# Clustered attention followed by an MLP on one core: a mask product and three ScalarE operations placed in other periods

## The chip, the cores and the metric

The kernel runs on one core of a Trainium2 chip. Its time is the device time of that core in microseconds, from launch to the last write. Before the change three runs were measured: 1022.56, 1022.64 and 1022.86 us. A further execution was recorded by the hardware profiler.

The core's engines each work through their own instructions in order and meet only through semaphores: TensorE (PE in the profile; its loading of weights is listed apart as PEld), VectorE (DVE), ScalarE (ACT), GpSimd (POOL), and SyncE (SP), which here only starts transfers.

## The reference

For 4 batches and 8 heads, 768 tokens with 64 values each, every query and every key is assigned to the nearest of 16 centroids of its head. A query may look only at keys with the same assignment. Then the result goes through an MLP with 2048 hidden values and the gate h * erf(softplus(h)).

```python
q_assign = np.argmax(np.einsum('bhsd,hcd->bhsc', q_n, c_n), axis=-1)
k_assign = np.argmax(np.einsum('bhsd,hcd->bhsc', k_n, c_n), axis=-1)
mask = q_assign[:, :, :, None] == k_assign[:, :, None, :]
scores = scale * np.matmul(q, k.transpose(0, 1, 3, 2))
scores = np.where(mask, scores, -1000000000.0)
scores = scores - np.max(scores, axis=-1, keepdims=True)
attn = np.exp(scores)
attn = attn / (np.sum(attn, axis=-1, keepdims=True) + 1e-09)
return np.matmul(attn, v).astype(np.float32)
...
h = x @ w_in
sp = np.maximum(h, 0.0) + np.log1p(np.exp(-np.abs(h)))
g = h * erf(sp)
return (g @ w_out).astype(np.float32)
```

## The kernel before

**Two parts.** The first part, up to about 430 us of the span, is the attention. The second is the MLP, made of products of 128x128 blocks into PSUM banks called `bank`. The change touches the first part only.

**Pairs and periods.** The attention runs over 16 pairs of heads (`p`, 0 to 15). The two heads of a pair lie on partitions 0 to 63 and 64 to 127, so most TensorE products come in twos: one contracts over rows 0 to 63 (`e` = 0), the next over rows 64 to 127 (`e` = 1). A pair has six periods (`i`, 0 to 5), and a period treats two units; a unit is 128 keys against half of the queries (384 of 768). `period(p, i)` (line 720) writes out the order by hand, and a wrapper class (`InOrder`, line 55) keeps every engine's instructions in the order in which the code calls them. All of them therefore carry line 63 in the profile, and the groups are told apart by their tiles.

**One period on TensorE**, in this order:

- in periods 0 and 3 `turn` (line 390): six small products that turn the row minima (`lowest`) into the bank `turned[h]`. Two ScalarE copies then write them as one row for each head into `qm`, the masks of the queries. `scores` read that row.
- `step_ahead` (line 711): a step of the row maxima for the pair ahead, four short bf16 products into `wide` (from `kv`, `qv`, then `km`, `qm`). VectorE reduces `wide` to `nmx`, and the next step writes the same `wide` again. From period 3 on these steps belong to the next pair.
- place 0 of a mask product (`mask(0)`).
- `products` (line 410) of the two units: `qT` times `kT` in f32 into a bank `sc`.
- place 1 of a mask product, and a second `step_ahead`.
- `scores` (line 423) of the two units: four short bf16 products of `km` and `qm` onto the same `sc`.
- place 2 of a mask product. Its copy by ScalarE stands between the `curve` of the first unit and that of the second.
- in period 3, `similarities` for the pair after the next, into `turned[1]`.
- `attend` (line 453) of the two units of the period before: `pr` times `in_v` into `turned[half]`. In the profile these are the `turned<-pr,in_v` products over all 128 rows.
- in periods 0 and 3 the beginning of `divide` (line 465): the sums of the weights (`minus` times the accumulated `pr`) into the other bank `turned[1 - half]`.

**Mask products.** `masks` (line 350) multiplies the one-hot assignments `hotT` with `pick`, over rows 0 to 63 for the queries and 64 to 127 for the keys, into a bank `turned`. ScalarE copies the result to `qm` (queries) or `km` (keys, with a bias). There are four per pair: two halves for each of queries and keys. The table `MASKS` (line 51) says in which period and place each stands, and for the pair after the current one; `FIRST_MASKS` is the same for pair 0. The bank is `turned[0]` in periods 0 and 5, `turned[1]` otherwise. Before, both key products stand in period 0, at places 1 and 2. The row maxima of the next pair read the second half of its `km` for the first time at the second `step_ahead` of period 3.

**ScalarE in a period** does the copies of the turn, the copy of a mask if there is one, two `curve` operations (the exponential from `sc` to `pr`), and then, in periods 0 and 3, the two operations of `divide`, Ln and Exp, which make `inv`. In the period that follows VectorE makes from them `den` (reading the bank of the sums), then the scaled accumulator, then, after a row maximum, the result `x`. The next `attend` writes the bank that `den` reads.

**The conversion.** The MLP's weights arrive as 64-bit numbers and are turned into f32 by integer and f32 operations, one piece of 512 columns at a time, 22 of 32 pieces during the attention: pieces 2p-1 and 2p in pair p (`n1`, `n2`; with none for -1). A piece takes `size_and_rest` (line 236, two ScalarE operations: Abs into `w_in`, and a scaled copy of the low word), `bounded` (VectorE), `sign` (line 245, ScalarE, written as int16 into the upper half of the low words), `shifted` (VectorE) and `summed` (line 253, POOL, which adds the parts and then fetches a later piece into the place that came free). `sign` follows the `size_and_rest` of its piece, and `summed` follows all.

**POOL** adds up the `pr` of each unit (`accumulate`) and runs `summed` in periods 1 and 4.

Of the kernel before, what the change touches and what calls it, by code (L numbers as in the profile page):

```python
# [47 lines left out]
NPT = NJ + 2  # L48
N_LATE = 10
LAST_X = 11  # L50
MASKS = {(0, 1): ("k", 0), (0, 2): ("k", 1), (2, 0): ("q", 0), (5, 0): ("q", 1)}
FIRST_MASKS = {(2, 0): ("k", 0), (2, 1): ("q", 0), (2, 2): ("k", 1), (5, 0): ("q", 1)}


# [17 lines left out]
def kernel(  # L72
# [163 lines left out]
    def size_and_rest(n):  # L236
        w, (hi, lo, _) = w_steps[n][0], steps[n]
        ae.activation(out=w, in_=hi, func=ACT.Abs, scale=UP)
        ae.activation(out=lo.bitcast(I32), in_=lo.bitcast(U32), func=ACT.Copy, scale=2.0**-29)

    def bounded(n):
        w = w_steps[n][0]
        ve.tensor_scalar(out=w, in0=w, scalar1=2.0, scalar2=None, op0=ALU.max)

    def sign(n):
        hi, _, upper = steps[n]
        ae.activation(out=upper, in_=hi, func=ACT.Prelu, scale=2.0**-25, alpha=2.0**90)

    def shifted(n):
        w = w_steps[n][0].bitcast(U32)  # L250
        ve.tensor_scalar(out=w, in0=w, scalar1=3, scalar2=None, op0=ALU.logical_shift_left)
# [59 lines left out]
    def similarities(p):  # L311

        if p >= NPAIR:
            return
        st = pairs[p]
        st["psim"] = turned[1][:, 0:HW]
        for g in range(4):
            te.matmul(
                st["psim"][2 * C * g : 2 * C * (g + 1)], lhsT=ccT[:, p % HP],
                rhs=st["qk"[g // 2] + "T"][:, (g % 2) * HW : (g % 2 + 1) * HW],  # L320
                start=True, stop=True,
            )

    def choose(p, spare=None):

        if p >= NPAIR:
            return
        st = pairs[p]
        n = HW // C
        sims = routep.tile([P, HW], F32, name="sims")  # L330
        ve.transpose(out=sims, in_=st.pop("psim"))
        yield
        sim = sims.rearrange("p (g c) -> p g c", c=C)
        mx = (wide[:, 0] if spare is None else spare)[:, 512 - n :]
        ve.reduce_max(out=mx, in_=sim, axis=AX.X)
        yield
        hot = routep.tile([P, HW], BF16, name="hot")
        ve.tensor_tensor(
            out=hot.rearrange("p (g c) -> p g c", c=C), in0=sim,
            in1=mx.unsqueeze(2).to_broadcast([P, n, C]), op=ALU.is_equal,  # L340
        )
        yield
        st["hotT"] = routep.tile([P, HW], BF16, name="hotT")
        ve.transpose(out=st["hotT"], in_=hot)
# [5 lines left out]
    def masks(p, nm, half, bank):  # L350

        if p >= NPAIR:
            return lambda: None
        st = pairs[p]
        cols = slice(half * HW, (half + 1) * HW)
        r = slice(0, D) if nm == "q" else slice(D, P)
        won = bank[:, 0:HW]
        te.matmul(won, lhsT=pick[r, half], rhs=st["hotT"][r], start=True, stop=True)
        if nm == "q":
            return lambda: ae.activation(out=st["qm"][:, cols], in_=won, func=ACT.Relu)  # L360
        return lambda: ae.activation(
            out=st["km"][:, cols], in_=won, func=ACT.Identity, bias=nbig, scale=BIG
        )
# [26 lines left out]
    def turn(p, h, copies=(ae.copy, ae.copy)):  # L390

        st = pairs[p]
        pn = turned[h][:, 0:HW].rearrange("p (t n) -> p t n", t=HJ)
        for t in range(HJ):
            for e in range(2):
                cols = slice(e * D, (e + 1) * D)
                te.matmul(pn[cols, t], lhsT=lowest[h][:, t, cols], rhs=identb, start=True, stop=True)
        for e, copy in zip(range(2), copies):
            r = slice(e * D + SH, e * D + SH + 1)
            copy(out=st["qm"][r, h * HW : (h + 1) * HW], in_=pn[r].rearrange("p t n -> p (t n)"))  # L400
        st["shift", h] = True
# [8 lines left out]
    def products(u):  # L410
        p, half, j = units[u]
        if u in sc_of:
            return
        st = pairs[p]
        sc = sc_of[u] = ps_s.tile([P, 2, 512], F32, name="sc", tag="s")
        for e in range(2):
            r = slice(e * D, (e + 1) * D)
            te.matmul(
                sc[:, e, 0:HW], lhsT=st["kT"][r, j * P : (j + 1) * P],
                rhs=st["qT"][r, half * HW : (half + 1) * HW], start=True, stop=False,  # L420
            )

    def scores(u):

        p, half, j = units[u]
        st = pairs[p]
        sc = sc_of[u]
        assert ("shift", half) in st
        for e in range(2):
            r = slice(e * D, (e + 1) * D)  # L430
            te.matmul(
                sc[:, e, 0:HW], lhsT=st["km"][r, j * P : (j + 1) * P],
                rhs=st["qm"][r, half * HW : (half + 1) * HW], start=False, stop=True,
            )

    def curve(u):

        pr = prs[u % NPT]
        ae.activation(out=pr[:, :, 0:HW], in_=sc_of.pop(u)[:, :, 0:HW], func=ACT.Exp, scale=D**-0.5)
# [265 lines left out]
    def run(work):  # L705
        for _ in work:
            pass
# [3 lines left out]
    def step_ahead(u):  # L711
        p, i = divmod(u + NJ, 2 * NJ)
        if p < NPAIR:
            maxima_step(p, i)
# [5 lines left out]
    def period(p, i):  # L720
        u = 2 * NJ * p + 2 * i
        n1, n2 = 2 * p - 1, 2 * p
        early = lambda n: 0 <= n < N_EARLY

        def mask(place):
            which = (MASKS if p else FIRST_MASKS).get((i, place))
            if which:
                return masks(p + 1, *which, turned[0 if i in (0, 5) else 1])
            return lambda: None

        if u > 0:
            for which in turns if i in (0, 3) else ():
                turn(*which)
                turns.remove(which)
            step_ahead(u)
        mask(0)()
        next(part[0], None)
        if u == 2:
            next(routing[0])
        products(u)  # L740
        products(u + 1)
        mask(1)()
        if u > 0:
            step_ahead(u + 1)
        next(part[0], None)
        scores(u)
        scores(u + 1)
        later = mask(2)
        if i == 3:
            similarities(p + 2)  # L750
            routing[0] = choose(p + 2)
        curve(u)
        later()
        curve(u + 1)
        if u == 0:
            step_ahead(1)
            similarities(1)
            routing[0] = choose(1, turned[0])
            next(routing[0])
            next(routing[0])  # L760
            vectors(1, "q")
            vectors(1, "k")
        if i == 0 and early(n1 - 1):
            shifted(n1 - 1)
        elif i == 1 and early(n1):
            size_and_rest(n1)
        elif i == 2 and early(n1):
            bounded(n1)
            sign(n1)
        elif i == 3:  # L770
            if early(n1):
                shifted(n1)
            if early(n2):
                size_and_rest(n2)
        elif i == 4 and early(n2):
            sign(n2)
        elif i == 5 and early(n2):
            bounded(n2)
        for work in forms[: FORMS.get(p, {}).get(i, 0)]:
            work()  # L780
            forms.remove(work)
        if i == 3:
            for _ in range(3):
                next(routing[0], None)
        if i == 0:
            if p:
                transposes(p + 2, "q")
        elif i == 1:
            load(p + 1, "v", v, vp)
            if p == 0:  # L790
                run(routing[0])
                transposes(2, "q")
        elif i == 2:
            transposes(p + 2, "k")
        elif i == 4:
            vectors(p + 2, "k")
        elif i == 5:
            run(routing[0])
            vectors(p + 2, "q")
        if u > 0:  # L800
            for w in (u - 2, u - 1):
                accumulate(w)
            if i == 1 and early(n1 - 1):
                summed(n1 - 1)
            elif i == 4 and early(n1):
                summed(n1)
            for w in (u - 2, u - 1):
                attend(w)
            if i % HJ == 0:
                part[0] = divide(u - 1)  # L810
                next(part[0])
        mask(3)()
# [178 lines left out]
```

## Time and profile before

| what | value |
|---|---|
| median of 3 runs | 1022.64 us (1022.56 to 1022.86) |
| profiled execution, its own time | 1022.77 us |
| its span, first to last instruction | 1021.1 us |
| granted TensorE clock | 1.00 |
| TensorE busy | 1013.9 us (99%) |
| VectorE busy | 695.8 us (68%) |
| ScalarE busy | 515.0 us (50%) |
| GpSimd busy | 345.7 us (34%) |
| one pair (149.10 to 175.49 us): TensorE, VectorE, ScalarE, GpSimd busy | 26.37, 19.84, 21.07, 19.93 us |
| one mask product on TensorE | 320 ns, 63 in all |
| the key masks' copy by ScalarE | 578 ns, 32 in all |
| sign by ScalarE | 1363 ns |
| size, rest by ScalarE | 681, 683 ns |
| exponential of a unit by ScalarE | 810 ns |

A line of the order of time has the start in us, the length in us, the engine, the line of the code, the operation, what it writes and reads, the shapes, and the number of instructions merged in it. In brackets stands the idle time of the engine before it and what ended it. The length of a short instruction includes its way through the engine, so that two that follow each other closely overlap in the record: matmuls of 0.32 us can start 0.16 us apart.

### The profile page before, as it was taken

To read this page: it belongs to the slowest core of one execution; us is meant where nothing else is said; L and a number is where in the kernel's file an instruction comes from. 1 tells how busy PE (TensorE), PEld (TensorE's weight loads), DVE (VectorE), ACT (ScalarE), POOL (GpSimd) and SP (SyncE) were. 2 spreads that over 40 slices of the span, in tenths; PEclk is the share of its full clock that TensorE was granted. 3 is DMA by queue.
4 is the path that set the end of the run, shared out by engine and by line. 5 is a ranking of instruction groups with operands and counts; after the bars stand their busy time and mean duration, and the time that the engine had idled before them with its cause. 6 is when DMAs were issued, how large, how long until landed. Compare 5 with 4: busy or idle time off the path is not lost.

```text
span 1021.1 us, 15464 instructions
## 1 busy us (share of the span) xinstructions
PE 1013.9 (99%) x5930; PEld 726.1 (71%) x5930; DVE 695.8 (68%) x1305; ACT 515.0 (50%) x673; POOL 345.7 (34%) x229
## 2 busy tenths in 40 slices
PE   8999999999999999999999999999999999999998
PEld 3555555554555445478888888888888888888887
DVE  8777777777777777778875674756565547565754
ACT  3787877787777666567615142322233141505050
POOL 1777777777777667745130000000000000000000
PEclk9999999999999999999999999999999999999999
DMA  9344444444343311041100100110011000000001
GB/s 214 68 98 97 104 104 103 104 104 104 83 104 87 76 28 32 24 154 61 42 1 21 63 1 1 42 42 1 1 41 42 1 21 22 1 1 21 21 1 41
DMA packets 141641, 55.55 MB, mean 54 GB/s; under 512 B 127104, under 2 KB 131456, under 8 KB 141568
## 3 DMA queue, kind: packets, MB, share of 16 engines
q1 hardware_dynamic: 139216, 54.28, 20.8%
q8 instruction: 46, 0.75, 0.3%
q10 hardware_dynamic: 2352, 0.30, 0.2%
q14 instruction: 27, 0.22, 0.1%
HBM read 41.98 MB, written 12.58 MB: 53 GB/s over the span
## 4 chain that ended last, share of the span: by engine, by line
PE 97%; DVE 1%; POOL 0%; ACT 0%; issue 0%; DVEq 0%; ACTq 0%; POOLq 0%
PE bank L63 43%; PE turned L63 33%; PE sc L63 15%; PE wide L63 7%; DVE nmx L63 1%; POOL more_out L63 0%; DVE sims L63 0%; ACT inv L63 0%; DVE kT L63 0%; DVE qT L63 0%; ACT pr L63 0%; DVE hotT L63 0%; DVE wide L63 0%; DVE den L63 0%; DVE hot L63 0%
## 5 line engine op out<-in xcount | busy, mean ns | idle before, releaser
L63 POOL TENSOR_TENSOR more_out<-more_out,pr 128x768 f32<-128x768 f32 x128 | 223.5, 1746 | 67.6 <-ACT pr L63 62.5
L63 DVE TENSOR_REDUCE nmx<-wide 128x2 f32<-128x768 f32 x189 | 180.7, 956 | 95.1 <-PE wide L63 70.8
L63 ACT ACTIVATE pr<-sc 128x768 f32<-128x768 f32 x192 | 147.0, 810 | 75.0 <-PE sc L63 75.0
L63 PE MATMUL turned<-pr,in_v 128*64 128x386 f32 x768 | 145.5, 500 | 0.1
L63 DVE TENSOR_TENSOR g<-bank,g 128x256 f32<-128x256 f32 x222 | 89.5, 421 | 52.9 <-PE bank L63 46.3
L63 PE MATMUL bank<-x_own,w_in 128*128 128x256 f32 x424 | 104.5, 380 | 0.0
L63 PE MATMUL bank<-w_out,g 128*128 128x256 f32 x448 | 103.1, 379 | 0.0
L63 PE MATMUL sc<-qT,kT 64*128 64x384 f32 x528 | 99.7, 484 | 0.0
L63 PEld LDWEIGHTS turned<-pr,in_v 128*64 128x64 f32 x768 | 46.7, 136 | 72.2 <-issue 71.1
L63 PEld LDWEIGHTS bank<-w_out,g 128*128 128x128 f32 x448 | 85.2, 190 | 11.5
L63 PEld LDWEIGHTS bank<-x_own,w_in 128*128 128x128 f32 x424 | 80.4, 190 | 12.1 <-issue 1.2
L63 ACT COPY g<-bank 128x256 f32<-128x256 f32 x28 | 10.4, 372 | 152.5 <-PE bank L63 148.5
L63 DVE TENSOR_TENSOR osb<-bank,osb 128x256 f32<-128x256 f32 x87 | 35.4, 420 | 72.8 <-ACT osb L63 25.4
L63 ACT ACT_TABLE_LOAD x48 | 61.6, 1283 | 45.7 <-DVE g L63 45.0
L63 POOL TENSOR_TENSOR more_out<-pr,pr 128x768 f32<-128x768 f32 x32 | 58.8, 1837 | 58.5 <-ACT pr L63 58.5
L63 PE MATMUL bank<-x_more,more_in 128*128 128x256 f32 x296 | 76.0, 379 | 0.0
L63 PEld LDWEIGHTS <-qv 64*128 64x128 bf16 x384 | 25.6, 93 | 65.2 <-issue 51.1
L63 PE MATMUL wide<-kv,qv 64*128 64x384 bf16 x378 | 69.4, 328 | 1.1 <-ACT km L63 0.6
L63 PEld LDWEIGHTS sc<-qT,kT 64*128 64x128 f32 x528 | 56.6, 187 | 16.6 <-issue 1.2
L63 PE MATMUL wide<-km,qm 64*128 64x384 bf16 x378 | 68.3, 322 | 0.0
L63 PE MATMUL bank<-more_out,g_more 128*128 128x256 f32 x272 | 64.3, 379 | 0.0
L63 DVE TENSOR_TENSOR g<-a_s,g 128x512 f32<-128x512 f32 x96 | 62.4, 688 | 1.4 <-ACT a_s L63 1.4
(162 smaller groups left out, 1710.2 us busy)
## 6 DMA issues: line engine op xcount, KB each, us to landing
x_own<-in_moe_w_in_dram SPq DMA_DIRECT2D x13, 512.0 KB, 4.3
in_v<-in_v_dram SPq DMA_DIRECT2D x32, 192.0 KB, 2.9
x_dram<-more_out SPq DMA_DIRECT2D x32, 192.0 KB, 2.4
x_own<-x_dram SPq DMA_DIRECT2D x6, 1024.0 KB, 5.1
out_dram<-osb SPq DMA_DIRECT2D x23, 256.0 KB, 2.0
in_k<-in_k_dram SPq DMA_DIRECT2D x59, 96.0 KB, 2.7
in_q<-in_q_dram SPq DMA_DIRECT2D x58, 96.0 KB, 3.6
g_more<-in_moe_w_out_dram SPq DMA_DIRECT2D x6, 512.0 KB, 3.6
```

The costliest lines, as they stand in the source:

```text
L63: ins = getattr(self.engine, name)(*args, **kw)
```

## The change

The keys' second mask product of the next pair moves from period 0, place 2, to period 2, place 2, for pairs 1 to 14 (pair 0 has its own table, and the last pair has no next). With the period it changes its bank from `turned[0]` to `turned[1]`. Its ScalarE copy moves along: from between the two exponentials of period 0 to between those of period 2.

Of the conversion only ScalarE's operations move. For the odd pieces (`n1`) `sign` goes from period 2 to period 3. For the even pieces (`n2`) `size_and_rest` goes from period 3 to period 4, and `sign` from period 4 to period 0 of the next pair, where it stands behind the exponentials and ahead of Ln. The VectorE and POOL operations stay where they are. Each engine has the same instructions as before; only the orders on TensorE and ScalarE differ.

```diff
-MASKS = {(0, 1): ("k", 0), (0, 2): ("k", 1), (2, 0): ("q", 0), (5, 0): ("q", 1)}
+MASKS = {(0, 1): ("k", 0), (2, 0): ("q", 0), (2, 2): ("k", 1), (5, 0): ("q", 1)}
...
         if i == 0 and early(n1 - 1):
             shifted(n1 - 1)
+            sign(n1 - 1)
         elif i == 1 and early(n1):
             size_and_rest(n1)
         elif i == 2 and early(n1):
             bounded(n1)
+        elif i == 3 and early(n1):
+            shifted(n1)
             sign(n1)
-        elif i == 3:
-            if early(n1):
-                shifted(n1)
-            if early(n2):
-                size_and_rest(n2)
         elif i == 4 and early(n2):
-            sign(n2)
+            size_and_rest(n2)
         elif i == 5 and early(n2):
             bounded(n2)
```

## The prediction

> **What bounds the kernel now.** I read the page first, then the chain of waits, then the order of time on TensorE and ScalarE through one pair.
>
> ```profile
> PE   8999999999999999999999999999999999999998
> ...
> PE 97%; DVE 1%; POOL 0%; ACT 0%; issue 0%; DVEq 0%; ACTq 0%; POOLq 0%
> ```
>
> TensorE sets the end: nine tenths busy in all slices but the ends, and 97% of the chain that ended last. But a busy share also counts slots in which a matmul stands spread out, so the losses have to be found in the distances between starts. In the order of time I marked the start of each period's 8 products `turned<-pr` ("attends"). For pair 5, attends of period 1 to attends of the next period 1, the steps are 3.98, 5.01, 4.46, 3.98, 4.50, 4.46 us, sum 26.39; pairs 1 to 11 all have this pattern within 0.02. So a saving per pair repeats. TensorE first, periods 0 and 2 of pair 5 (start, us, engine, line, operation, count):
>
> ```profile
> 151.36 0.63 PE L63 MATMUL sc<-qm,km 64*128 64x384 bf16 x4
> 152.01 0.32 PE L63 MATMUL turned<-hotT,pick 64*128 64x384 bf16 x1
> 152.26 1.52 PE L63 MATMUL turned<-pr,in_v 128*64 128x386 f32 x8
> ...
> 158.50 0.32 PE L63 MATMUL turned<-hotT,pick 64*128 64x384 bf16 x1
> 158.51 1.61 PE L63 MATMUL sc<-more_out 64*128 64x384 f32 x8
> 159.80 0.48 PE L63 MATMUL wide<-kv,qv 64*128 64x384 bf16 x2
> 159.96 0.48 PE L63 MATMUL wide<-km,qm 64*128 64x384 bf16 x2
> 160.12 0.64 PE L63 MATMUL sc<-qm,km 64*128 64x384 bf16 x4
> 160.70 1.52 PE L63 MATMUL turned<-pr,in_v 128*64 128x386 f32 x8
> 162.04 0.34 PE L63 MATMUL turned<-identb,lowest 128*64 128x128 bf16 x6
> ...
> 164.27 0.73 PE L63 MATMUL sc<-qm,km 64*128 64x384 bf16 x4
> ```
>
> Then ScalarE in the same stretch:
>
> ```profile
> 151.38 0.58 ACT L63 ACTIVATE km<-turned,nbig 128x384 bf16<-128x384 f32 x1 [0.41 <-PE turned L63]
> 151.92 0.81 ACT L63 ACTIVATE pr<-sc 128x768 f32<-128x768 f32 x1
> 152.63 0.58 ACT L63 ACTIVATE km<-turned,nbig 128x384 bf16<-128x384 f32 x1
> 153.09 0.81 ACT L63 ACTIVATE pr<-sc 128x768 f32<-128x768 f32 x1
> 154.53 0.58 ACT L63 ACTIVATE inv<-turned,alleps 128x384 f32<-128x384 f32 x1 [0.62 <-PE turned L63]
> ...
> 160.71 1.52 ACT L63 ACTIVATE pr<-sc 128x768 f32<-128x768 f32 x2 [0.97 <-PE sc L63]
> 162.11 1.37 ACT L63 ACTIVATE x_more<-x_more 128x512 int16<-128x512 f32 x1
> 163.50 0.97 ACT L63 CAST qm<-turned 1x384 bf16<-1x384 f32 x2
> ```
>
> Two losses are to be seen. In period 0 the second mask product starts at 152.01, just after ScalarE has read the first one out of the same bank (151.38+0.58=151.96). In period 3 the scores from 164.27 take 0.73 instead of 0.49 (period 1, at 156.30): they read the shift rows of `qm`, whose copies run from 163.50 to 164.47, behind the sign operation of 1.37.
>
> **Period 0: the keys' second mask leaves.** The last scores start at 151.36+0.63-0.32=151.67. From the last short matmul to the attends it is 0.26 elsewhere (period 2: 160.12+0.64-0.32=160.44, then 160.70). So without the mask the attends start at 151.93, not 152.26: 0.33. Cross-check: the step into period 0 of pair 15, which has no successor and so no masks, is 3.99 against 4.50; a mask that costs one slot of 0.16 leaves 0.35 for the other. This happens for pairs 1 to 14: 14 x 0.33 = 4.6 us.
>
> **Period 0: the sign enters on ScalarE, pairs 1 to 11.** It stands between the second `pr` and the Ln of the division. Before, `km` stood there (0.46 from its start to the next `pr`). New: `pr` 151.92, `pr` 0.70 later (half of 156.73 to 158.12) at 152.62, sign at 153.32. How soon may Ln follow a sign? Nearest rows: sign then a full-width copy, 171.58 to 172.66, 1.08; sign then the one-row copies, 1.39. Ln has 128 partitions, so I take 1.08: Ln at 154.40. TensorE would let it start at 154.53-0.33=154.20. What is late next: before, from Ln's start to `den` it is 1.24 (155.77), to the end of `den` 1.79, to the end of `x` 3.63 (157.62+0.54). Attends of period 1 wait for `den` (the bank), the queries' mask of period 2 waits for `x` (the other bank). With 0.05 for a semaphore (151.96 to 152.01) the attends, wanted at 156.39, need Ln by 154.55; that mask, wanted 1.78 later, needs it by 154.49. So 154.40 is hidden with 0.09 to spare. With 1.39 Ln starts at 154.71 and 0.22 is lost per pair, 11 x 0.22 = 2.4 us; that is the upper end, the lower end nothing. The row-maximum after them has until 154.6. VectorE's first row-maximum there (154.89 before) is over by then. POOL's sum of that weight piece ran at 155.75, after the sign's new end (153.32+1.37=154.69), so the next fetch on SP's queue is not held.
> The Trainium skill, "ScalarE: Activation LUTs", section What ACT_TABLE_LOAD costs, lets back-to-back operations overlap by about 93 ns only, less than the 0.28 of the row here; by it Ln would start at 154.60, an estimate, and 0.1 per pair (1.2 us) would be lost. I go by the row.
>
> **Period 2: the keys' mask comes in behind the scores.** One slot is 0.16 (matmul starts at 159.80, 159.96, 160.12). Does it lengthen TensorE's work? Here the rows decide. The queries' mask at 158.50 uses array rows 0 to 63, and the next product's first half, on the same rows, follows in program order; yet a product starts at 158.51, not 158.66. From there the pairs stand staggered (0.48 for two `wide`, 0.33 in period 1), and of the two at 159.80 and 159.96 the trace has the semaphore wait on the later one, which the program gives to the first half. So the half on rows 64 to 127 has run past and leads by one slot. It ends its last score at 160.44, exactly when the other half begins its last. The keys' mask uses rows 64 to 127: it fits into that hole, and the attends stay at 160.70. Cost 0. Lower end 0 (nothing is removed here), upper end 0.16 for a slot, or 0.25 by the distance from mask to attends in period 0 (152.01 to 152.26): 14 x 0.25 = 3.5 us.
> Against this stands the Trainium skill, "TensorE: Matmul & The Clock Gate", Part 3, The mechanism: matmuls start and end strictly in program order. If that held across row halves, the first half would have started at 158.66 with its partner beside it, and the mask would cost its slot, some 2 us in all. The staggered rows contradict it here.
>
> On ScalarE the mask's copy `km` stands between the two `pr`. In pair 0, which already does so (28.66 `pr`, 29.36 `km`, ended 29.93, `pr` 29.83), it ended 1.27 after the first `pr`: here 161.98. The turn of the minima at 162.04 writes that same bank and now waits for it: 162.03. Covered by 0.01; each 0.1 that `pr` is later would cost 14 x 0.1. Behind the turn stands all of period 3. ScalarE is idle 0.97 before that `pr`, so I book nothing. The second `pr` is 0.47 later, at 161.88; its bank is wanted by the second pair of products near 163.4, POOL comes to it at 163.5. The row-maxima that first read the new `km` stand at 163.94. The queries' copy at 159.26 is out of the bank long before 160.44.
>
> **Period 3: the sign leaves period 2, pairs 1 to 11.** The second `pr` ends at 161.88+0.81=162.69, the `qm` copies run to 163.66, and the scores at 164.27 find them ready: 0.73 becomes 0.49, 0.24 each. Pair 0, with no sign there, makes the step in 4.77 against 5.01: the same 0.24. 11 x 0.24 = 2.6 us. Pairs 12 and 13 have no sign; their step of 4.88 carries VectorE's preparing subtractions instead and stays.
>
> **Edits at no cost.** Period 3 gets the sign for size and rest (from `pr` to Ln 1.40+1.08=2.48, at most 2.79, within the 2.99 from 164.93 to 167.92). Period 4 gets size and rest for the sign (1.14 to the next copy against 1.08; the wait of 0.20 for scores in period 5, at 174.16, covers 0.06). The limiting operation on VectorE stays in period 5, over two microseconds after its input. No DMA is moved.
>
> **Sum.** 4.6+2.6=7.2 us off the profiled execution's 1022.77 (span 1021.1, 1.7 around it): 1015.5; the median of the runs is 0.13 lower, so 1015.4. After the attention TensorE is the bound again and nothing waits for a clock time, so the gain passes through.
>
> **Rivals.**
> 1. Ln waits for the whole sign: +2.4, so 1017.8. For it: the 1.39 row. Against: that follower is a copy of one partition, and such copies also follow each other with no overlap (two in 0.97).
> 2. The keys' mask takes a slot: +0.16 x 14 = 2.2, less 0.2 that pairs 12 and 13 return (VectorE's lateness of 0.11 there is covered): 1017.4; at 0.25, 1018.7. For it: program order. Against: the staggered starts.
> 3. Slower: ScalarE becomes the bound in period 0. If the second `pr` stays at 153.09 and nothing overlaps, sign starts at 153.90, Ln at 155.29, 0.80 after the limit: 11 x 0.80 - 7.2 = +1.6, 1024.2. It decides from Ln at about 155.14 (0.65 per pair). For it: ScalarE's new chain has no idle left there. Against: that `pr` followed `km` by 0.46 without idle, so `km` was what held it.
> 4. 1 and 2 together, or small waits at the turn: 1019.7 to 1021.2.
>
> **Chances.** Forecast 0.64 (own range 1014.8 to 1016.4), rival 1 0.15, rival 2 0.10, rival 3 0.04, rival 4 0.07. The measurement can tell about 0.2%, 2 us, from no change, so faster means below 1020.6: 0.64+0.15+0.10 and half of rival 4, 0.92; same 0.04; slower 0.04. The range 1014.6 to 1018.9 leaves out rivals 3 and 4 and a little more.
>
> **What would show it.** Attend steps of pairs 1 to 11 at 3.98, 4.77, 4.46, 3.98, 4.17, 4.46. Right if the step over period 0 falls by 0.33 and the next does not grow (rival 1 adds 0.22 to it or to the step into period 2); if the step into period 2 stays 3.98 (rival 2: 4.14) with a mask starting at the last score; if the scores of period 3 take 0.49. Wrong if Ln follows the sign after more than 1.2, or if the turn after period 2 starts over 1.4 after its attends.

## The result, and the profile after

The changed kernel takes 1015.52 us (median of 6 runs, 1015.43 to 1015.64), against 1022.76 us for the kernel before (6 runs, 1022.56 to 1022.86): ratio 0.9930, 95% interval 0.9917 to 0.9942. The forecast was 1015.4.

The page of the changed kernel, its TensorE row in 40 slices and its chain by engine:

```profile
PE   8999999999999999999999999999999999999998
...
PE 97%; DVE 1%; DMA 1%; POOL 0%; ACT 0%; SPq 0%; issue 0%; DVEq 0%; ACTq 0%; POOLq 0%
```

Neither line shows the gain. TensorE's row has the same digits as before, and its share of the chain is again 97%; TensorE was the bound and still is. The gain is in the distances between the attends (starts of each period's `turned<-pr` in the order of time):

| step of the attends, pairs 1 to 11 | before | forecast | after |
|---|---|---|---|
| period 1 to 2 | 3.98 | 3.98 | 3.98 |
| period 2 to 3 | 5.01 | 4.77 | 4.78 |
| period 3 to 4 | 4.46 | 4.46 | 4.46 |
| period 4 to 5 | 3.98 | 3.98 | 3.98 |
| period 5 to 0 | 4.50 | 4.17 | 4.16 |
| period 0 to 1 | 4.46 | 4.46 | 4.46 |

The rows are taken as typical of these pairs; they differ by up to 0.02 from pair to pair. Before rounding the step into period 3 fell by 0.225 in the mean (5.010 to 4.785). 14 x 0.34 for period 0 and 11 x 0.225 for period 3 are 7.2 us, and the span fell from 1021.1 to 1013.8. The rest of the kernel kept its length (587.2 us from the last attends to the end in both), so the gain passed through whole. Of the span's 7.3 us, 0.17 is not the change's: the first attends stand at 24.56 instead of 24.73, ahead of everything that was moved.

TensorE after the change, periods 0 and 2 of pair 5 (start, us, engine, line, operation, count):

```profile
148.96 0.63 PE L63 MATMUL sc<-qm,km 64*128 64x384 bf16 x4
149.51 1.52 PE L63 MATMUL turned<-pr,in_v 128*64 128x386 f32 x8
...
155.76 0.32 PE L63 MATMUL turned<-hotT,pick 64*128 64x384 bf16 x1
155.77 1.61 PE L63 MATMUL sc<-more_out 64*128 64x384 f32 x8
157.06 0.48 PE L63 MATMUL wide<-kv,qv 64*128 64x384 bf16 x2
157.22 0.48 PE L63 MATMUL wide<-km,qm 64*128 64x384 bf16 x2
157.38 0.64 PE L63 MATMUL sc<-qm,km 64*128 64x384 bf16 x4
157.71 0.32 PE L63 MATMUL turned<-hotT,pick 64*128 64x384 bf16 x1
157.96 1.52 PE L63 MATMUL turned<-pr,in_v 128*64 128x386 f32 x8
159.31 0.35 PE L63 MATMUL turned<-identb,lowest 128*64 128x128 bf16 x6
...
161.54 0.49 PE L63 MATMUL sc<-qm,km 64*128 64x384 bf16 x4
```

In period 0 the attends follow the scores by 0.55, before by 0.90. In period 2 the keys' mask starts at 157.71, together with the last score of the other half of the rows (157.38+0.64-0.32=157.70), and the attends stand 0.58 behind the scores, exactly as before without it: the product costs nothing here. The scores of period 3 take 0.49.

ScalarE in the same stretch:

```profile
148.97 0.58 ACT L63 ACTIVATE km<-turned,nbig 128x384 bf16<-128x384 f32 x1 [0.41 <-PE turned L63]
149.52 1.51 ACT L63 ACTIVATE pr<-sc 128x768 f32<-128x768 f32 x2
150.92 1.37 ACT L63 ACTIVATE x_own<-x_own 128x512 int16<-128x512 f32 x1
152.01 0.59 ACT L63 ACTIVATE inv<-turned,alleps 128x384 f32<-128x384 f32 x1
...
157.97 0.81 ACT L63 ACTIVATE pr<-sc 128x768 f32<-128x768 f32 x1 [0.96 <-PE sc L63]
158.68 0.57 ACT L63 ACTIVATE km<-turned,nbig 128x384 bf16<-128x384 f32 x1
159.14 0.81 ACT L63 ACTIVATE pr<-sc 128x768 f32<-128x768 f32 x1
159.98 0.97 ACT L63 CAST qm<-turned 1x384 bf16<-1x384 f32 x2
```

Ln (152.01) follows the sign after 1.09. There is no idle time ahead of it any more, where before there was 0.62, so ScalarE now sets its start; yet the attends of period 1 did not move. In period 2 the mask's copy ends at 158.68+0.57=159.25, 0.06 ahead of the turn at 159.31. The turn does not start later for it: in the trace it stands 1.348 after its attends, before and after. But its six products are spread a little more, 0.134 instead of 0.118 from the first start to the last. That is the 0.016 by which period 3 missed its forecast.

### The profile page after: what moved, and what is told of

The parts are those of the page before. It is cut to its first block, busy times and chain, and to the rows that moved or that the text cites. A ratio compares the mean times of both kernels' runs of the same rounds, so it can differ in the third digit from the quotient of the medians.

```text
span 1013.8 us, 15440 instructions
## 1 busy us (share of the span) xinstructions
PE 1006.4 (99%) x5930; PEld 724.0 (71%) x5930; DVE 695.5 (69%) x1305; ACT 513.5 (51%) x673; POOL 346.5 (34%) x229
## 4 chain that ended last, share of the span: by engine, by line
PE 97%; DVE 1%; DMA 1%; POOL 0%; ACT 0%; SPq 0%; issue 0%; DVEq 0%; ACTq 0%; POOLq 0%
PE bank L63 43%; PE turned L63 32%; PE sc L63 15%; PE wide L63 7%; DVE nmx L63 1%; POOL more_out L63 0%; DMA in_k<-in_k_dram 0%; DMA in_q<-in_q_dram 0%; DVE kT L63 0%; SPq L63 0%; DVE sims L63 0%; ACT inv L63 0%; DVE qT L63 0%; ACT pr L63 0%; DVE den L63 0%
```

## The experiments

Times of the kernel before beside them differ a little from batch to batch: 1022.58 (24 runs) for the first four kernels, 1023.02 (13) for the next two, 1022.72 (9) for the last three.

**The mask alone**, ScalarE's sign and size operations left in their old periods:

```diff
-MASKS = {(0, 1): ("k", 0), (0, 2): ("k", 1), (2, 0): ("q", 0), (5, 0): ("q", 1)}
+MASKS = {(0, 1): ("k", 0), (2, 0): ("q", 0), (2, 2): ("k", 1), (5, 0): ("q", 1)}
```

> Only the keys' second mask product moves to period 2; ScalarE's sign and size operations stay where they were before. Theory (the two parts need each other): period 0 gains 0.33 for pairs 1 to 14, but in period 2 ScalarE now does exponential, mask copy, exponential and then the sign, so the sign starts 0.47 later, the copies of the shift rows end 0.47 later, and the scores of period 3 wait 0.47 longer for pairs 1 to 11: -4.6 + 5.2 = +0.6, about 1023.3 us. The step of attends into period 3 is about 5.48 instead of 5.01, the one into period 0 is 4.17. Rival (the parts add up, the mask move is worth its slot and wait by itself): 4.6 off, 1018.1 us, step into period 3 unchanged at 5.01.

Measured: 1022.95 us (1022.89 to 1023.03), ratio 1.0003, interval 0.9994 to 1.0013: no gain at all. The steps are 4.16 into period 0, as in the full change, but 5.47 into period 3. Periods 2 and 3 of pair 5 on ScalarE, then the scores of period 3 on TensorE:

```profile
160.64 0.81 ACT L63 ACTIVATE pr<-sc 128x768 f32<-128x768 f32 x1 [0.96 <-PE sc L63]
161.34 0.57 ACT L63 ACTIVATE km<-turned,nbig 128x384 bf16<-128x384 f32 x1
161.81 0.81 ACT L63 ACTIVATE pr<-sc 128x768 f32<-128x768 f32 x1
162.50 1.37 ACT L63 ACTIVATE x_more<-x_more 128x512 int16<-128x512 f32 x1
163.89 0.96 ACT L63 CAST qm<-turned 1x384 bf16<-1x384 f32 x2
```

```profile
164.41 0.32 PE L63 MATMUL sc<-qm,km 64*128 64x384 bf16 x1
164.90 0.48 PE L63 MATMUL sc<-qm,km 64*128 64x384 bf16 x3 [0.18 <-ACT qm L63]
```

The mask's copy pushes the sign back, the sign pushes the copies of the shift rows to 164.85, and the second product of the scores starts only at 164.90. What period 0 gains (14 x 0.34 = 4.8) period 3 gives back (11 x 0.46 = 5.1).

**ScalarE's part alone**, with both masks of keys left in period 0:

```diff
-MASKS = {(0, 1): ("k", 0), (2, 0): ("q", 0), (2, 2): ("k", 1), (5, 0): ("q", 1)}
+MASKS = {(0, 1): ("k", 0), (0, 2): ("k", 1), (2, 0): ("q", 0), (5, 0): ("q", 1)}
```

(against the changed kernel)

> Only ScalarE's sign and size operations move; both key masks stay in period 0. Theory: the scores of period 3 lose their wait, 0.24 for pairs 1 to 11, 2.6 us off. In period 0 the sign now comes on top of the second mask copy, Ln starts near 154.88 on the clock of pair 5 before, where the limit of the queries' mask is then 154.82, so 0.06 is lost per pair: 1022.76 - 2.6 + 0.6 = 1020.7 us. Step into period 3 at 4.77, into period 0 at 4.50. Rival (the parts add up): 1020.1 us; and if the sign needs its whole 1.37 before Ln, another 3 us are lost: 1023.8.

Measured: 1020.09 us (1020.02 to 1020.24), ratio 0.9976, interval 0.9966 to 0.9985. Steps: 4.77 into period 3, 4.50 into period 0, and 3.99 to 4.00 into period 2. So the gain of period 3 is there in full; of the 0.06 that I expected to be lost behind Ln only 0.01 to 0.02 show, and the total falls on the number of the rival. The limit for Ln was drawn some 0.04 too tight. The two parts alone bring +0.4 and -2.5 us, together -7.2: they do not add, and the difference of 5 us is the wait of 0.46 in period 3 that the mask alone creates and ScalarE's part removes.

**The keys' mask of period 2 issued twice**, against the changed kernel:

```diff
-        te.matmul(won, lhsT=pick[r, half], rhs=st["hotT"][r], start=True, stop=True)
+        for _ in range(2 if p > 1 and (nm, half) == ("k", 1) else 1):
+            te.matmul(won, lhsT=pick[r, half], rhs=st["hotT"][r], start=True, stop=True)
```

> The changed kernel, with the keys' mask product of period 2 issued twice in a row (the second writes the same values into the same bank) for pairs 1 to 14. Theory (the first fits into the hole that the leading half of the array rows leaves; there is one slot of it and no more): the second costs a slot of 0.16, 14 x 0.16 = 2.2 us less 0.2 that pairs 12 and 13 give back: 1017.5 us, step into period 2 at 4.14. Rival (a short product behind the scores is hidden anyway, in the time that TensorE needs before the attends over all rows): no change, 1015.5 us, step at 3.98.

Measured: 1017.44 us (1017.33 to 1018.44), ratio 0.9953, interval 0.9936 to 0.9970; step into period 2 at 4.14, and the step into period 3 of pairs 12 and 13 at 4.77 in place of 4.87. TensorE in period 2 of pair 5:

```profile
157.97 0.64 PE L63 MATMUL sc<-qm,km 64*128 64x384 bf16 x4
158.30 0.48 PE L63 MATMUL turned<-hotT,pick 64*128 64x384 bf16 x2
158.72 1.52 PE L63 MATMUL turned<-pr,in_v 128*64 128x386 f32 x8
```

From scores to attends it is now 0.75, not 0.58. The first product is free, the second costs its slot of 0.16 to 0.17. The hole holds one.

**The queries' mask taken out of period 2**, against the changed kernel:

```diff
-MASKS = {(0, 1): ("k", 0), (2, 0): ("q", 0), (2, 2): ("k", 1), (5, 0): ("q", 1)}
+MASKS = {(0, 1): ("k", 0), (0, 2): ("q", 0), (2, 2): ("k", 1), (5, 0): ("q", 1)}
```

> The changed kernel, with the queries' first mask moved out of period 2 to period 0, place 2, so that the keys' mask is alone in period 2 and no half of the rows leads there. Theory (hole): the keys' mask now costs its slot, step into period 2 at 3.98 as with the queries' mask alone; in period 0 the queries' mask waits for the copy of the first key mask out of the same bank as the second key mask did before, step into period 0 at 4.50, 14 x 0.33 = 4.6 us, and Ln comes close to its limit: 1020.1 to 1020.8 us. Rival (a product behind the scores is hidden anyway): step into period 2 at 3.82, 2.2 us less: 1017.9 us.

Measured: 1020.05 us (1020.01 to 1020.23), ratio 0.9975, interval 0.9966 to 0.9985. Step into period 2 at 3.98, into period 0 at 4.50; in pairs 1 and 4 the step into period 3 is longer (4.94 and 4.90) because an exponential starts late there, 0.3 us in all. Period 2 of pair 5:

```profile
159.25 0.49 PE L63 MATMUL sc<-qm,km 64*128 64x384 bf16 x4
159.58 0.32 PE L63 MATMUL turned<-hotT,pick 64*128 64x384 bf16 x1
159.83 1.52 PE L63 MATMUL turned<-pr,in_v 128*64 128x386 f32 x8
```

The scores stand in step again (0.49 for four), the mask starts after the last of them (159.25+0.49-0.32=159.42, plus a slot of 0.16), and the period costs as much with the keys' mask alone as it did with the queries' mask alone, or with both. What a period without any mask takes is to be seen in pair 15, which has no successor; its attends of periods 1 and 2 in the changed kernel are 3.82 apart:

```profile
411.53 1.52 PE L63 MATMUL turned<-pr,in_v 128*64 128x386 f32 x8
415.35 1.52 PE L63 MATMUL turned<-pr,in_v 128*64 128x386 f32 x8
```

So the mask is not free for standing behind the scores; it was free where the other half of the rows had been delayed by a slot. That is what separates the theory from its rival.

**The two masks of period 2 swapped**, against the changed kernel:

```diff
-MASKS = {(0, 1): ("k", 0), (2, 0): ("q", 0), (2, 2): ("k", 1), (5, 0): ("q", 1)}
+MASKS = {(0, 1): ("k", 0), (2, 0): ("k", 1), (2, 2): ("q", 0), (5, 0): ("q", 1)}
```

> The changed kernel, with the two masks of period 2 swapped: the keys' mask (rows 64 to 127) at place 0, the queries' (rows 0 to 63) behind the scores. Theory: the hole is symmetric; now rows 0 to 63 lead and the queries' mask fills what they leave. Step into period 2 stays 3.98; ScalarE's copy between the exponentials is the shorter one (0.49 for 0.57), so the turn loses its last 0.01: 1015.3 to 1015.5 us. Rival (products start in the order of the program, and the keys' mask was free for another reason, its rows): the queries' mask costs 0.16, 1017.5 us, step at 4.14.

Measured: 1015.49 us (1015.24 to 1015.70), ratio 0.9927, interval 0.9910 to 0.9943; steps 3.98 and 4.77. End of period 2 of pair 5:

```profile
157.57 0.33 PE L63 MATMUL sc<-qm,km 64*128 64x384 bf16 x2
157.74 0.32 PE L63 MATMUL turned<-hotT,pick 64*128 64x384 bf16 x1
157.74 0.32 PE L63 MATMUL sc<-qm,km 64*128 64x384 bf16 x1
157.99 1.52 PE L63 MATMUL turned<-pr,in_v 128*64 128x386 f32 x8
```

Mask and last score start together again, now with the halves exchanged. Which of the two leads does not matter.

**One more copy on ScalarE ahead of Ln in period 0**, against the changed kernel:

```diff
+        if half == 1 and 2 * p < N_EARLY:
+            ae.copy(out=inv, in_=st["kT"][:, 0:HW])
         ae.activation(out=inv, in_=psum, func=ACT.Ln, bias=alleps, scale=-1.0)
```

> The changed kernel, with one more ScalarE copy of 128x384 ahead of Ln in period 0 of pairs 1 to 11 (it writes the tile that Ln overwrites). Theory: Ln has 0.09 to spare in the changed kernel; the copy makes it later by 0.45 (copies overlapping) to 0.60 (Ln waiting for the whole copy), of which 0.36 to 0.51 reach TensorE as a wait of the attends of period 1 for den and of the queries' mask of period 2 for x: 11 x that = 4.0 to 5.6 us, 1019.5 to 1021.1 us. Rival (ScalarE has room in period 0, and what follows hides it): 1015.5 to 1016.

Measured: 1022.33 us (1022.09 to 1022.47), ratio 0.9994, interval 0.9985 to 1.0003. The direction is the theory's, the size is above its range: 6.8 us, 0.62 per pair. Steps: 4.90 into period 1 (+0.44), 4.16 into period 2 (+0.18). ScalarE, then TensorE, in periods 0 to 2 of pair 5:

```profile
153.74 1.37 ACT L63 ACTIVATE x_own<-x_own 128x512 int16<-128x512 f32 x1
154.84 0.59 ACT L63 COPY inv<-kT 128x384 f32<-128x384 f32 x1
155.46 0.58 ACT L63 ACTIVATE inv<-turned,alleps 128x384 f32<-128x384 f32 x1
```

```profile
157.24 1.52 PE L63 MATMUL turned<-pr,in_v 128*64 128x386 f32 x8 [0.37 <-DVE den L63]
...
159.09 0.32 PE L63 MATMUL turned<-hotT,pick 64*128 64x384 bf16 x1
159.10 1.60 PE L63 MATMUL sc<-more_out 64*128 64x384 f32 x8
160.50 0.37 PE L63 MATMUL wide<-kv,qv 64*128 64x384 bf16 x2
...
161.15 0.32 PE L63 MATMUL turned<-hotT,pick 64*128 64x384 bf16 x1
161.40 1.52 PE L63 MATMUL turned<-pr,in_v 128*64 128x386 f32 x8
```

Ln came 0.62 after the copy started, so it waited for the whole of it, and the attends of period 1 waited for `den`: that is the expected chain. The queries' mask at 159.09 stands 1.85 behind these attends, not 1.78: the wait for `x`, 0.07. What I had left out is the last 0.11: after that wait the two halves are only 0.05 apart (two `wide` in 0.37, not 0.48), the hole is nearly closed, and the keys' mask costs most of its slot. So rival 3 of the prediction describes a real limit. The change stays clear of it by about 0.1: in it `x` ends 0.16 ahead of the queries' mask, and here, where the mask waits, 0.05; for `den` and the attends it is 0.23 and 0.05. And 0.62 of further work on ScalarE takes the whole gain away.

**A step further.** If a mask of keys is free where it shares a period with a mask of queries, the two that still stand alone (keys' first in period 0, queries' second in period 5) can be put together too. The core of the edit, against the changed kernel:

```diff
-MASKS = {(0, 1): ("k", 0), (2, 0): ("q", 0), (2, 2): ("k", 1), (5, 0): ("q", 1)}
+MASKS = {(2, 0): ("q", 0), (2, 2): ("k", 1), (5, 0): ("q", 1), (5, 2): ("k", 0)}
...
-                return masks(p + 1, *which, turned[0 if i in (0, 5) else 1])
+                return masks(p + 1 + ((i, place) == (5, 2)), *which, turned[0 if i in (0, 5) else 1])
...
+        if i == 4:
+            vectors(p + 2, "k")
+        elif i == 1 and p:
+            vectors(p + 1, "q")
         curve(u)
```

with `hotT` in two buffers, all of `choose` in period 3, and the copies `vectors` gone from their old places. Beside it ran the changed kernel once more, and the same edit with `vectors` left behind the exponentials.

> The changed kernel once more, on the same chip as the two that follow, for comparison: 1015.5 us.

> A version beyond the change: the keys' first mask goes from period 0, place 1, to place 2 of period 5 of the pair before, behind the queries' second mask at place 0, so that both masks of keys fill a hole that a mask of queries opens. For that the assignments hotT get two buffers and are made in period 3, and the bf16 copies by ScalarE go ahead of the exponentials: those of the keys in period 4, those of the queries in period 1 of the next pair. Theory (one slot for each pair of masks, one of queries and one of keys): the step into period 0 falls from 4.16 to 3.99 for pairs 1 to 14, the step into period 5 stays 3.98; 14 x 0.17 = 2.4 us less than the changed kernel, 1013.1 us. Rival (the second mask of period 5 waits for the copy of the first out of the same bank, or ScalarE becomes late somewhere): gain eaten, 1015 us or more.

> The same with ScalarE's bf16 copies left where they were, behind the exponentials of periods 4 and 5. Theory: in period 5 the copy of the queries' mask then ends 0.12 after the hole begins, so the keys' mask and the attends are 0.12 later (step into period 5 at 4.1), and the copies of the shift rows in period 0 end 0.12 after the scores want them (step into period 0 at 4.1), for pairs 1 to 11: 0.24 x 11 = 2.6 us more than the version before, 1015.7 us. Rival (ScalarE has room there): 1013.1 us, as the version before.

Measured: the changed kernel 1015.49 us (1015.44 to 1015.74); all masks paired 1013.73 us (1013.66 to 1013.79), ratio to the kernel before 0.9912, interval 0.9899 to 0.9926; with the copies left late 1015.91 us (1015.89 to 1016.11), ratio 0.9934, interval 0.9922 to 0.9946. In the paired version the step into period 0 is 4.00 and the one into period 5 stays 3.98: 14 x 0.16 = 2.2 us. Period 5 of pair 5 in the paired version, then with the copies left late:

```profile
170.10 0.64 PE L63 MATMUL sc<-qm,km 64*128 64x384 bf16 x4
170.43 0.32 PE L63 MATMUL turned<-hotT,pick 64*128 64x384 bf16 x1
170.68 1.52 PE L63 MATMUL turned<-pr,in_v 128*64 128x386 f32 x8
```

```profile
170.92 0.65 PE L63 MATMUL sc<-qm,km 64*128 64x384 bf16 x4
171.32 0.32 PE L63 MATMUL turned<-hotT,pick 64*128 64x384 bf16 x1
171.57 1.52 PE L63 MATMUL turned<-pr,in_v 128*64 128x386 f32 x8
```

In the first the mask starts with the last score and the attends stand 0.58 behind the scores, as in period 2 of the change; in the second the mask starts 0.40 behind the scores instead of 0.33, and the attends 0.65. Some 0.3 us of the gain go again in 0.02 to 0.03 per pair on the way into period 2, and 0.3 us in pair 1, where an exponential starts 0.28 late and the turn with it; why it starts late was not tried, and the same step is long with the copies left late too (5.11). So the time missed the expected 1013.1 by 0.6. With the copies left late the steps into periods 5 and 0 are about 4.06 and 4.09 in pairs 1 to 11, 0.08 and 0.09 longer where 0.12 was expected. In pairs 12 to 14, where no loss was expected, the step into period 0 is 4.17. The paired version is the fastest of all, 1.8 us ahead of the change.

## Why the prediction was right

**The likeliest case came true, and by its own steps.** The step into period 0 fell by 0.34 (0.33 forecast), the one into period 3 by 0.225 (0.24), all others stayed within 0.01, and the sum missed the median by 0.1 us. That it came so close is partly luck: period 0 brought 4.7 us for 4.6, period 3 2.5 for 2.6, and the 0.17 ahead of the first attends was in no term.

**The second mask leaves period 0.** Confirmed: 4.16 wherever it left (the full change, and the mask alone), 4.50 wherever a second mask waits for the copy of the first out of the same bank, a keys' mask (ScalarE's part alone) or a queries' one (the queries' mask taken away). With no mask in period 0, in the paired version, the step is 4.00, so the mask that is left costs its slot of 0.16. The other 0.18 of the 0.34 is put down to the wait for the bank by the order of time alone (the second mask starts 0.05 after the copy ends); a second mask there in another bank was not tried.

**The hole in period 2.** This was the step in dispute. The measured 3.98 alone would not have proved it, since a product behind the scores might have been hidden anyway. Twice the mask (4.14) and the mask without its counterpart (3.98, when 3.82 is a period with no mask) exclude that, and the swap shows the symmetry. The rule of the Trainium skill ("TensorE: Matmul & The Clock Gate", Part 3, The mechanism) that matmuls start strictly in program order, by which some 2 us would have gone, does not hold here between halves of the rows.

**Ln behind the sign.** 1.09 for the 1.08 taken from the row of the full-width copy. The figure of the Trainium skill ("ScalarE: Activation LUTs", What ACT_TABLE_LOAD costs), an overlap of about 93 ns, by which 0.1 per pair would have gone, does not fit: here it is 0.28. The spare time that I had worked out as 0.09 was a little larger, 0.11 by the distance from `x` to the mask: with both mask copies ahead of it, Ln stood some 0.05 behind my limit and cost only 0.01 to 0.02.

**The turn, covered by 0.01.** It was the thinnest cover in the sum. The turn started on time, 1.348 after its attends, with the copy ended 0.06 before, yet its products were spread by 0.016 more, which the sum had not counted. With the masks swapped, the shorter copy stands there and ends 0.15 before the turn, the products keep their 0.118, and the step is 4.77.

**The scores of period 3.** 0.73 became 0.49, as in pair 0. The mask alone shows the price of the old place: with the sign still in period 2 the same scores would have waited 0.46 longer. The prediction treated the two parts as two gains; it did not say that the larger one can't be had without the other.

## What to carry to other kernels

Where products use halves of the array's rows, count the slots of each half, not of TensorE: here an extra product on one half opened a hole on the other, and a second one there was free, once, with its bank free by then. When work is moved between stretches, check what stands behind it on its new engine; here each part alone brought nothing or a third, and both together brought all. A busy share of 99% hides losses that the distances between like instructions show.

## What the runs showed of the hardware

Two halves of the rows can change order: of two `wide` products in period 2 the one that the program issues second starts 0.16 earlier (157.06 and 157.22; the wait that belongs to the first issued is on the later one), and that half stays ahead through eight f32 products and eight short ones. The lead did not release a reader too soon. The last issued of the four `wide` products carries the signal for VectorE and starts at 157.22, its partner of the other half at 157.38; VectorE's row maximum starts at 157.75, 0.37 after the partner, the same distance as from the last product in a period without a lead. So it was in all 29 steps of that trace in which the half with the signal led. Nor is the lead fixed: in the kernel with one more copy the leading half's first f32 product after a wait took 0.59 instead of 0.48 in the record, and the lead was 0.05; why is not shown. On ScalarE the overlap of two operations was not one number: 0.28 between the sign (1.37 long, followed after 1.09) and Ln, 0.11 between two exponentials (0.81, followed after 0.70), and none where Ln overwrote the tile of the copy ahead of it (0.59, followed after 0.62).
